# Products of an attention stage moved from 128 by 128 to 64 by 64 TensorE tiles, in a fused attention and feed-forward kernel

## The chip, the cores and the metric

The kernel runs on one core of one Trainium2 chip. A core has TensorE (PE; its weight loads are listed as PEld), VectorE (DVE), ScalarE (ACT), GpSimd (POOL) and SyncE (SP), which here only issues transfers. Each engine works through its own instructions in the order in which the program gives them. The metric is the device time of one execution in microseconds (us). A profiled execution leaves a trace; times of single instructions come from it.

## The reference

Eight batches of eight heads, 576 positions, 64 features each. q is normalised by a softmax over the features, k by one over the positions; kv = k^T v is a 64 by 64 matrix per head, and the attention's output is q kv. The heads' outputs side by side form x, 4608 rows by 512. Then comes a feed-forward part with a sine:

```python
k_s = np.exp(k - max_over_seq(k)); k_s = k_s / sum_over_seq(k_s)
q_s = np.exp(q - max_over_d(q));   q_s = q_s / sum_over_d(q_s)
kv = np.einsum('bhsd,bhse->bhde', k_s, v)
attn = np.einsum('bhsd,bhde->bhse', q_s, kv)
x = attn.transpose(0, 2, 1, 3).reshape(4608, 512)
h = x @ w_in                       # 512 by 2048
g = h + np.sin(alpha * h)**2 / (alpha + 1e-9)
out = g @ w_out                    # 2048 by 512
```

Inputs and output are float32 in HBM.

## The kernel before

**Feed-forward part.** The 4608 rows are worked through in nine tiles t of 512 rows. A tile has 16 slots (ni), one for each 128 columns of h. In a slot, `mm_h` makes four products of 128 by 512 (one for each 128-row chunk ki of w_in) into one PSUM bank, written hp; `sine` has ScalarE take the sine of it and the square; `combine` has VectorE form g from the square and from hp, which leaves the bank free. A later slot that is given the same bank waits for that combine. The order of the banks is written out: `BANKS` for tiles 0 to 2, and "aabb" repeated after that, where a and b are pools of two banks each. Each 512-row tile then needs 64 products with w_out (`mm_o`, four accumulations of 16), which `o_stream` hands out one by one: between two slots of tile t, `take(os, n)` puts n products of tile t-1 on TensorE's queue. After each 16 of them `evac_o` has VectorE copy the result out of PSUM and SP store it.

**Attention part.** While tile t = b-1 is worked through (for t from 3 to 6), batch b is prepared between its slots: exps of q and k on ScalarE before slot 0; normalising q on GpSimd; the transposed q (`qT`) by a transfer at slot 3; at slot 5 `kv_mm` with 72 small products on 64 by 64 tiles, then `kv_norm` on VectorE; and at slots 9, 11, 13 and 15 the products x = q kv (`attn_out`), each with a copy by VectorE into `xT`, the transposed x from which `mm_h` reads. xT is a ring of 2560 columns. Earlier batches are prepared in stretches of their own, with `attn_chunk`: batch 0 at the start, batch 1 after tile 0, batch 2 after tile 1; batch 3 is prepared in tile 2. A position s is j + 9p, with nine j of 64 positions.

**The x products before.** The 64 by 64 kv matrices of two heads stand on the diagonal of a 128 by 128 matrix (`kbd`), whose other blocks are set to zero once. One product of the full array then makes a chunk of x for two heads, of which half of the multiplications are by zeros. A batch has four chunks c = (ii, e) of 576 columns. `attn_out` makes the two chunks of one ii for four or five j: two products of 256 or 320 columns and one VectorE copy of 512 or 640 columns.

Of the kernel before, what the change touches and what calls it, by code (L numbers as in the profile page):

```python
# [15 lines left out]
F32 = mybir.dt.float32  # L16
BF16 = mybir.dt.bfloat16
AX = mybir.ActivationFunctionType
ALU = mybir.AluOpType
# [4 lines left out]
def kernel(  # L24
# [14 lines left out]
    nc = tc.nc  # L39
    ctx.enter_context(nc.allow_non_contiguous_dma(reason="layout"))  # L40
    B, H, S, D = q.shape
# [3 lines left out]
    J = 9  # L45
    P = S // J
    nN = d_ff // 128
    MF = 512
# [3 lines left out]
    NX = 5 * MF  # L52

    ctx.enter_context(tc.manual_schedule())
    singles = ctx.enter_context(tc.tile_pool(name="singles", bufs=1))
# [12 lines left out]
    xT = singles.tile([128, 4, NX], BF16, name="xT")  # L68
    q8 = singles.tile([128, 4, 2, D], F32, name="q8")
    win = singles.tile([128, 4, d_ff], BF16, name="win")  # L70
# [1 line left out]
    alpha_rows = singles.tile([nN, 128], F32, name="alpha_rows")  # L72
    alpha_sb = singles.tile([128, nN], F32, name="alpha_sb")
    inva_sb = singles.tile([128, nN], F32, name="inva_sb")
    kbd = [singles.tile([128, 2, 2, 128], BF16, name=f"kbd{n}") for n in range(2)]
    vb = [singles.tile([128, J, 4 * 65], BF16, name=f"vb{n}") for n in range(2)]

    def src_view(t, b):
        return t[b].rearrange("(i e) (p j) d -> (e p) i (j d)", e=2, j=J)

    win_v = moe_w_in.rearrange("(x c d) n -> x d c n", x=2, c=4)
    wout_v = moe_w_out.rearrange("(no ni) d -> ni no d", ni=128)
    out_v = out.rearrange("(b p j) d -> b j p d", b=B, j=J)

# [30 lines left out]
    A = {}  # L115
# [48 lines left out]
    def kv_mm(b, ii, pool, split=False):  # L164

        if ii == 0 or split:
            A["kvp", b] = pool.tile([128, 2, 512], F32, name="kvp", tag="a")
        kvp, ke, vt = A["kvp", b], A["ke", b], vb[b % 2]
        for j in range(J):
            for x in range(2):  # L170
                h = 2 * ii + x
                for e in range(2):
                    r = slice(64 * e, 64 * e + 64)
                    nc.tensor.matmul(kvp[64 * x:64 * x + 64, e, ii * 65:(ii + 1) * 65],  # L174
                                     ke[r, j, h * 64:(h + 1) * 64],
                                     vt[r, j, h * 65:(h + 1) * 65],
                                     start=(j == 0), stop=(j == J - 1))

    def kv_norm(b, i0=0, i1=2):

        kt, m = kbd[b % 2], i1 - i0
        kvr = small.tile([128, 2, 2], F32, name="kvr")[:, :, 0:m]
        src = A["kvp", b][:, :, i0 * 65:i1 * 65].rearrange("p e (ii c) -> p e ii c", ii=m)
        nc.vector.reciprocal(kvr, src[:, :, :, D])
        for x in range(2):
            r = slice(64 * x, 64 * x + 64)
            nc.vector.tensor_tensor(kt[r, :, i0:i1, r], src[r, :, :, 0:D],  # L187
                                    kvr[r].unsqueeze(3).to_broadcast([64, 2, m, D]), op=ALU.mult)

    def q_tile(b):  # L190
        if ("qT", b) not in A:
# [20 lines left out]
                in_ = in_.rearrange("p j c -> p (j c)")  # L212
            nc.sync.dma_start(out=out, in_=in_, transpose=True)

    XO = ((0, 4), (4, 9))

    def attn_out(b, ii, half, pool, eng):
        qT, kt = A["qT", b], kbd[b % 2]
        j0, j1 = XO[half]
        n = (j1 - j0) * P  # L220
        xp = pool.tile([128, 2, 512], F32, name="xp", tag="a")
        for e in range(2):
            nc.tensor.matmul(xp[:, e, 0:n], kt[:, e, ii], qT[:, ii, j0:j1, e * 64:(e + 1) * 64],  # L223
                             start=True, stop=True)
        c0 = (J * b + j0) * P % NX
        eng(xT[:, 2 * ii:2 * ii + 2, c0:c0 + n], xp[:, :, 0:n])  # L226

    def attn_chunk(b, c, j0, j1, xp):

        ii, e = divmod(c, 2)  # L230
        nc.tensor.matmul(xp, kbd[b % 2][:, e, ii], A["qT", b][:, ii, j0:j1, e * 64:(e + 1) * 64],
                         start=True, stop=True)


    G = {}

    HP = {}
    BANKS = {0: "aabbkllaabbkllaa", 1: "kbbllaakbbllaabb", 2: "aabbooaabbooaabb"}

    def bank(kind):  # L240

        if kind == "k":
            return ps_k.tile([128, 2, MF], F32, name="kvp", tag="a")[:, 0]
        pool = {"a": lambda: ps_h[0], "b": lambda: ps_h[1], "l": lambda: ps_l, "o": lambda: ps_o}[kind]()
        return pool.tile([128, MF], F32, name={"l": "lp", "o": "op"}.get(kind, "hp"), tag=kind)

    def mm_h(t, ni, k0=0, k1=4):

        if ni == 0 and k0 == 0:
            G[t] = gpool.tile([128, nN, MF], BF16, name="g")  # L250
        hp = HP[t, ni] if k0 else bank(BANKS.get(t, 4 * "aabb")[ni])
        HP[t, ni] = hp
        for ki in range(k0, k1):
            nc.tensor.matmul(hp, win[:, ki, ni * 128:(ni + 1) * 128],  # L254
                             xT[:, ki, t * MF % NX:t * MF % NX + MF], start=(ki == 0), stop=(ki == 3))
        return hp

    def sine(t, ni, hp, sq):
# [48 lines left out]
    zero = singles.tile([128, 1], F32, name="zero")  # L307
    nc.vector.memset(zero, 0.0)
    for n in range(2):
        nc.vector.memset(kbd[n], 0.0)  # L310
        nc.vector.memset(vb[n].rearrange("p j (i c) -> p j i c", i=4)[:, :, :, D:D + 1], 1.0)

    ps_h = [ctx.enter_context(tc.tile_pool(name=f"ps_{n}", bufs=2, space=PSUM, reuse_waits="tile")) for n in "ab"]
# [67 lines left out]
    cast_v0(1, 5, 9, DVE_CP)  # L381

    xp = [bank("b") for _ in range(2)]
    for c in range(2):
        attn_chunk(0, c, 0, 8, xp[c])
    DVE_CP(xT[:, 0, 0:MF], xp[0])
    ACT_CP(xT[:, 1, 0:MF], xp[1])
    ACT_CP(A["qT", 0][:, 1, 0:8], tp1)
    nc.scalar.activation(zero, zero, AX.Sin)
    kv_mm(0, 1, ps_k, split=True)  # L390
# [1 line left out]
    for ki in range(2):  # L392
        for ni in range(2):
            mm_h(0, ni, ki, ki + 1)
    for c in range(2, 4):
        xp = bank("l")
        attn_chunk(0, c, 0, 8, xp)
        DVE_CP(xT[:, c, 0:MF], xp)
    for ki in range(2):
        for ni in range(2, 4):  # L400
            mm_h(0, ni, ki, ki + 1)
# [21 lines left out]
    def take(it, n=1000):  # L423
        for _ in range(n):
            if next(it, 0) == 0:
                return
# [4 lines left out]
    with ES:  # L431
# [47 lines left out]

        def x_half(ii):  # L480
            xp = [bank("a") for _ in range(2)]
            for e in range(2):
                attn_chunk(1, 2 * ii + e, 0, 8, xp[e])
            for e in range(2):
                (ACT_CP, DVE_CP)[e](xT[:, 2 * ii + e, MF:2 * MF], xp[e])

        kv_mm(1, 0, ps_k, split=True)
        kv_norm(1, 0, 1)
# [23 lines left out]
        def late_q8(ni):  # L512
            if ni == 11:
                tp = ps_k.tile([128, 2, 2, 128], BF16, name="tp", tag="a")
                for b in range(2):
                    for ii in range(2):
                        nc.tensor.transpose(tp[:, ii, b], A["qe", 1][:, J - 2 + b, ii * 128:(ii + 1) * 128], identb)
                DVE_CP(A["qT", 1][:, :, J - 2:J], tp)
            elif ni == 15:
                xp = ps_k.tile([128, 4, 2, P], F32, name="xp", tag="a")  # L520
                for c in range(4):
                    ii, e = divmod(c, 2)
                    for b in range(2):
                        nc.tensor.matmul(xp[:, c, b], kbd[b][:, e, ii],
                                         A["qT", 1][:, ii, J - 2 + b, e * 64:(e + 1) * 64], start=True, stop=True)
                DVE_CP(xT[:, :, 16 * P:18 * P], xp.rearrange("p c b n -> p c (b n)"))

        for ni in range(nN):
            h_slot(1, ni, SQ[ni], lag)
# [33 lines left out]
    norm_q(3, [GP])  # L563
    take(os, 20)

    c0 = J * 2 * P
    for c in range(4):
        xp = bank("aabb"[c])[:, 0:6 * P]
        attn_chunk(2, c, 0, 6, xp)
        (ACT_CP, DVE_CP)[c % 2](xT[:, c, c0:c0 + 6 * P], xp)  # L570
        take(os, 3 if c == 1 else 1)
    xp = ps_a.tile([128, 2, 512], F32, name="xp", tag="a")[:, :, 0:6 * P]
    for c in range(4):
        attn_chunk(2, c, 6, 9, xp[:, c // 2, (c % 2) * 3 * P:(c % 2 + 1) * 3 * P])
    DVE_CP(xT[:, :, c0 + 6 * P:c0 + 9 * P].rearrange("p (h c) n -> p h c n", h=2),
           xp.rearrange("p h (c n) -> p h c n", c=2))
    take(os)
    q_transpose_dma(3)
    load_batch(4)

    def attn_back(b, n, engs=4 * (DVE_CP,), xs=(4, 6, 8, 10)):
        if n == 0:
            kv_mm(b, 0, ps_a)
            kv_mm(b, 1, ps_a)
            kv_norm(b)
        elif n in xs:
            m = xs.index(n)
            attn_out(b, m // 2, m % 2, ps_a, engs[m])

    SQ2 = "PAPPAPAPPAPAPPAP"  # L590
    for ni in range(nN):
        h_slot(2, ni, SQ2[ni], lag)
        flush(lag, 2)
        attn_back(3, ni - 5, (DVE_CP, ACT_CP, ACT_CP, DVE_CP), (4, 6, 8, 10))
    flush(lag, 0)

    for t in range(3, nT):
        b = t + 1 if t + 1 < B else None
        os = o_stream(t - 1)
        done = 0  # L600
        if b is not None:

            exp_q(b)
            exp_k(b)
            cast_v(b, [GP_CP, GP_CP])
            norm_q(b, [GP])
            take(os, 8)
            done = 8
        for ni in range(nN):
            hp = mm_h(t, ni)  # L610
            if b is not None:
                if ni == 3:
                    q_transpose_dma(b)
                    if b + 1 < B:
                        load_batch(b + 1)
                attn_back(b, ni - 5)
            s = sine(t, ni, hp, "A")
            combine(t, ni, hp, s)
            want = 23 + 2 * (t == 3) + 21 * ni // 8 if b is not None else 4 * (ni + 1)
            take(os, min(64, want) - done)  # L620
            done = min(64, want)
        take(os)
# [36 lines left out]
```

## Time and profile before

| | us |
|---|---|
| median of three runs | 284.75 |
| the three runs | 284.06, 284.75, 286.88 |
| the profiled execution | 283.85 |
| its span, first to last instruction | 282.1 |

| stretch of the span, us | length | TensorE busy | VectorE | ScalarE | GpSimd |
|---|---|---|---|---|---|
| start, 0 to 16 | 16.00 | 9.81 | 10.32 | 11.33 | 9.91 |
| batch 1 in preparation, 36 to 46 | 10.00 | 9.66 | 8.44 | 6.61 | 0.95 |
| batch 2 in preparation, 66 to 75.9 | 9.90 | 9.85 | 9.69 | 7.39 | 7.06 |
| tile 2, 75.9 to 93.3 | 17.40 | 17.24 | 13.14 | 15.29 | 12.28 |
| one loop of tiles 3 to 6, 178.93 to 208.35 | 29.42 | 29.16 | 20.51 | 27.30 | 4.21 |
| tile 7, 208.35 to 236 | 27.65 | 27.49 | 14.97 | 20.83 | 0.00 |

How to read it: busy times of engines overlap, so a row does not add up to its length. A line of a group or of a timeline names the engine, the source line, the operation, what it writes and reads, the shape and the count; an entry in brackets is the time for which the engine stood idle before it, and what ended that. Products on TensorE are pipelined: a record of a 512-column product lasts 0.379 us, while a new one starts every 0.217 us. The granted clock of TensorE is 1.00 in every stretch but the last. Some products have no record.

### The profile page before, as it was taken

Reading aid. Unit: us, or ns where it says so; the run is one execution under the profiler, and the core shown is the slowest. Engines: PE = TensorE matmul, PEld = TensorE weight load, DVE = VectorE, ACT = ScalarE, POOL = GpSimd, SP = SyncE. Lnnn points to the kernel's source line nnn. Section 1 sums busy time; section 2 is a strip of 40 time slices with the busy share of each in tenths; the row PEclk is TensorE's granted clock in tenths of the full one; section 3 lists DMA queues with packets and bytes.
Section 4 is the critical chain, followed back from the end, with each engine's and each line's share of the span. In section 5 each row is a group of like instructions: output and inputs, shape, how many; then the busy total and the mean of one; then the engine's idle time right before and its main releaser. Section 6 shows DMA issues by size and latency. Waiting matters only on the chain.

```text
span 282.1 us, 4812 instructions
## 1 busy us (share of the span) xinstructions
PE 270.1 (96%) x1826; PEld 128.0 (45%) x1855; DVE 188.7 (67%) x288; ACT 225.5 (80%) x322; POOL 83.8 (30%) x80
## 2 busy tenths in 40 slices
PE   1999999999999999999999999999999999999994
PEld 0444444444444444444444444444444444444443
DVE  3968768899967768766875677567775555555412
ACT  3989576999589999899989998999877777777400
POOL 1988421877676550115003500340000000000000
PEclk9999999999999999999999999999999999999998
DMA  7999999996599039811992099109011111111143
GB/s 252 310 173 221 280 332 322 358 345 243 124 224 393 10 68 329 305 37 38 266 386 50 22 283 388 27 18 160 6 34 37 37 40 37 37 38 43 42 104 74
DMA packets 39127, 45.80 MB, mean 162 GB/s; under 512 B 17072, under 2 KB 22464, under 8 KB 39104
## 3 DMA queue, kind: packets, MB, share of 16 engines
q1 hardware_dynamic: 33360, 40.57, 46.9%
q0 software_dynamic: 5552, 4.79, 10.4%
q8 instruction: 14, 0.23, 0.3%
q10 hardware_dynamic: 192, 0.14, 0.2%
q14 instruction: 9, 0.07, 0.1%
HBM read 36.71 MB, written 9.44 MB: 164 GB/s over the span
## 4 chain that ended last, share of the span: by engine, by line
PE 84%; DMA 6%; ACT 3%; DVE 2%; POOL 1%; issue 1%; SPq 1%; ACTq 0%
PE op L274 38%; PE hp L254 37%; DMA st_v<-in_v_dram 6%; PE xp L223 2%; PE kvp L174 2%; PE lp L254 2%; POOL s L264 1%; PE op L629 1%; PE op L254 1%; ACT s L260 1%; PE kvp L254 1%; ACT vb L329 1%; DVE g L270 1%; SPq L299 1%; SPq L445 0%
## 5 line engine op out<-in xcount | busy, mean ns | idle before, releaser
L270 DVE SCALAR_TENSOR_TENSOR g<-s,inva_sb,hp 128x512 bf16<-128x512 f32 x128 | 94.1, 745 | 58.1 <-ACT s L262 52.6
L254 PE MATMUL hp<-xT,win 128*128 128x512 bf16 x507 | 127.9, 379 | 0.4
L274 PE MATMUL op<-wout,g 128*128 128x512 bf16 x477 | 121.6, 379 | 1.4 <-issue 0.6
L260 ACT ACTIVATE s<-hp,alpha_sb 128x512 f32<-128x512 f32 x128 | 86.3, 682 | 22.9 <-PE hp L254 21.2
L254 PEld LDWEIGHTS <-win 128*128 128x128 bf16 x576 | 56.0, 98 | 67.5 <-issue 1.3
L274 PEld LDWEIGHTS <-g 128*128 128x128 bf16 x560 | 54.0, 98 | 61.0 <-DVE g L270 0.3
L262 ACT ACTIVATE s<-s 128x512 f32<-128x512 f32 x112 | 70.5, 630 | 3.5
L264 POOL TENSOR_TENSOR s<-s 128x512 f32<-128x512 f32 x29 | 30.4, 1063 | 20.0 <-ACT s L260 19.9
L153 POOL TENSOR_TENSOR qn<-qe,qs 128x1152 bf16<-128x1152 bf16 (+1 forms) x12 | 25.1, 2109 | 34.1 <-DVE qs L147 22.7
L286 DVE COPY o<-op 128x512 f32<-128x512 f32 (+2 forms) x33 | 22.1, 668 | 9.9 <-PE op L274 5.5
L138 POOL CAST vb<-st_v 128x1152 bf16<-128x1152 f32 x12 | 14.7, 1257 | 45.3 <-DMA st_v<-in_v_dram 45.3
L119 ACT ACTIVATE qe<-st_q 128x1152 bf16<-128x1152 f32 (+2 forms) x18 | 17.7, 1025 | 6.7 <-DMA st_q<-in_q_dram 6.6
L119 ACT ACTIVATE ke<-st_k 128x1152 bf16<-128x1152 f32 x16 | 17.9, 1151 | 1.2 <-DMA st_k<-in_k_dram 1.2
L146 DVE TENSOR_REDUCE qs<-qe 128x36 f32<-128x2304 bf16 x5 | 12.8, 2553 | 7.9 <-ACT qe L119 7.9
L226 DVE CAST xT<-xp 128x512 bf16<-128x512 f32 (+1 forms) x18 | 13.5, 749 | 0.0
L119 ACT ACT_TABLE_LOAD x7 | 9.0, 1283 | 1.3 <-PEq L643 1.2
L274 PE MATMUL lp<-wout,g 128*128 128x512 bf16 x31 | 8.8, 379 | 0.2 <-issue 0.2
L274 PE MATMUL hp<-wout,g 128*128 128x512 bf16 x30 | 8.6, 379 | 0.1
L223 PE MATMUL xp<-qT,kbd 128*128 128x256 bf16 (+1 forms) x40 | 8.2, 286 | 0.0
L174 PEld LDWEIGHTS <-ke 64*64 64x64 bf16 x576 | 5.8, 108 | 4.6 <-ACT ke L119 0.8
L187 DVE TENSOR_TENSOR kbd<-kvp,kvr 64x256 bf16<-64x256 f32 (+1 forms) x20 | 7.4, 369 | 0.5
L254 PE MATMUL lp<-xT,win 128*128 128x512 bf16 x30 | 7.5, 379 | 0.1
(86 smaller groups left out, 135.0 us busy)
## 6 DMA issues: line engine op xcount, KB each, us to landing
out_dram<-o SPq DMA_DIRECT2D x70, 128.0 KB, 2.4
st_q<-in_q_dram SPq DMA_DIRECT2D x6, 1152.0 KB, 6.7
st_k<-in_k_dram SPq DMA_DIRECT2D x6, 1152.0 KB, 8.8
st_v<-in_v_dram SPq DMA_DIRECT2D x6, 1152.0 KB, 11.4
st_k<-in_k_dram SPq DMA_DIRECT2D x4, 576.0 KB, 7.5
st_q<-in_q_dram SPq DMA_DIRECT2D x4, 512.0 KB, 6.1
st_v<-in_v_dram SPq DMA_DIRECT2D x3, 576.0 KB, 8.0
wout<-in_moe_w_out_dram POOLq DMA_DIRECT2D x3, 512.0 KB, 10.3
```

The source lines that it names most:

```text
L119: nc.scalar.activation(dst[:, :, ii * 128:(ii + 1) * 128].rearrange("p j (x d) -> p x j d", x=2), src[:, ii::2], AX.Exp)
L138: engs[ii](vv[:, 2 * ii:2 * ii + 2, :, 0:D], staged["v", b][:, ii::2])
L153: engs[ii % len(engs)].tensor_tensor(qn[:, ii, 0:j1].rearrange("p j (x d) -> p j x d", x=2), qe[:, ii], part.unsqueeze(3).to_broadcast([12 ...
L223: nc.tensor.matmul(xp[:, e, 0:n], kt[:, e, ii], qT[:, ii, j0:j1, e * 64:(e + 1) * 64], start=True, stop=True)
L226: eng(xT[:, 2 * ii:2 * ii + 2, c0:c0 + n], xp[:, :, 0:n])
L254: nc.tensor.matmul(hp, win[:, ki, ni * 128:(ni + 1) * 128], xT[:, ki, t * MF % NX:t * MF % NX + MF], start=(ki == 0), stop=(ki == 3))
L260: nc.scalar.activation(s, hp, AX.Sin, scale=alpha_sb[:, ni:ni + 1])
L262: nc.scalar.activation(s, s, AX.Square)
L264: nc.gpsimd.tensor_tensor(s, s, s, op=ALU.mult)
L270: nc.vector.scalar_tensor_tensor(G[t][:, ni], in0=s, scalar=inva_sb[:, ni:ni + 1], in1=hp, op0=ALU.mult, op1=ALU.add)
L274: nc.tensor.matmul(acc, G[t][:, ni, j * 128:(j + 1) * 128], wout[:, ni, :], start=(ni == 0), stop=(ni == nN - 1))
L286: eng(o[:, cols], acc)
```

## The change

- `kbd` holds the two kv matrices above each other, 128 by 64 for each (e, ii), without zeros; `kv_norm` is one VectorE instruction on 128 partitions in place of two on 64, and the memsets of kbd go.
- `attn_x` makes x with four products on 64 by 64 tiles, one for each half x of the rows and each e of the columns. The two row halves write into two banks. The chunks of x are thereby other pairs of heads: chunk 2x+ii holds e = 0 and 1. The rows of w_in are loaded in the order that goes with it, and `KO` has `mm_h` take the chunks in the order in which they are made.
- Eight of the nine j make 512 columns, one bank. The ninth is made by `last_j` apart: eight products of 64 columns and one VectorE copy.
- Batches 4 to 7: the x products of slots 9, 11, 13 and 15 become one group of eight at slot 11. Its four banks are the two of pool a, lent, and the two of the pool that kv and x have used. Slots 12 and 13 use pool b in place of a, so the order of banks from slot 8 on is a a b b b b a a, for all tiles from 3 on. The copies are four VectorE instructions of 512 columns, two at slot 11, one each at slots 12 and 13; where the ring ends inside a batch (batch 4), each is split into two. The ninth group of batches 3 to 6 is made at slot 5 of the next loop, directly behind kv, in a part of kv's bank; that of batch 7 at slot 14.
- Batch 3 has a group of four at slots 9 and 13, batch 2 two groups of four (the second with the ninth group), batch 1 two and batch 0 two; the first of batch 0 stands directly ahead of a kv.

In the built program, VectorE's order in tiles 4 to 6 is: combine of slot 10, an output copy, two x copies, combine of slot 11, an x copy, combine of slot 12, an x copy, combine of slot 13. In tile 3 the output copy stands ahead of the combine of slot 10, and the x copies are twice as many. The first product of slot 12 waits for the combine of slot 10, that of slot 13 for the combine of slot 11. The orders of GpSimd and of SP are as before.

```diff
-    kbd = [singles.tile([128, 2, 2, 128], BF16, name=f"kbd{n}") for n in range(2)]
+    kbd = [singles.tile([128, 2, 2, D], BF16, name=f"kbd{n}") for n in range(2)]
-    win_v = moe_w_in.rearrange("(x c d) n -> x d c n", x=2, c=4)
+    win_v = moe_w_in.rearrange("(c x d) n -> x d c n", x=2, c=4)
...
-        for x in range(2):
-            r = slice(64 * x, 64 * x + 64)
-            nc.vector.tensor_tensor(kt[r, :, i0:i1, r], src[r, :, :, 0:D],
-                                    kvr[r].unsqueeze(3).to_broadcast([64, 2, m, D]), op=ALU.mult)
+        nc.vector.tensor_tensor(kt[:, :, i0:i1], src[:, :, :, 0:D],
+                                kvr.unsqueeze(3).to_broadcast([128, 2, m, D]), op=ALU.mult)
...
+    def attn_x(b, ii, j0, j1, outs):
+
         for e in range(2):
-            nc.tensor.matmul(xp[:, e, 0:n], kt[:, e, ii], qT[:, ii, j0:j1, e * 64:(e + 1) * 64],
-                             start=True, stop=True)
+            for x in range(2):
+                r = slice(64 * x, 64 * x + 64)
+                nc.tensor.matmul(outs[x][64 * e:64 * e + 64], kbd[b % 2][r, e, ii],
+                                 A["qT", b][r, ii, j0:j1, e * 64:(e + 1) * 64], start=True, stop=True)
...
+    def x_copy(eng, c, b, xp):
+
+        n0 = min(8 * P, NX - J * b * P % NX)
+        for n, m in ((0, n0), (n0, 8 * P)):
+            if n < m:
+                d0 = (J * b * P + n) % NX
+                eng(xT[:, c, d0:d0 + m - n], xp[:, n:m])
+
+    def last_j(b, xn):
+
+        for ii in range(2):
+            attn_x(b, ii, J - 1, J, [xn[:, x, ii * P:(ii + 1) * P] for x in range(2)])
...
+    KO = (0, 2, 1, 3)
...
-        hp = HP[t, ni] if k0 else bank(BANKS.get(t, 4 * "aabb")[ni])
+        hp = HP[t, ni] if k0 else bank(BANKS.get(t, 3 * "aabb" + "bbaa")[ni])
...
-        nc.vector.memset(kbd[n], 0.0)
...
+    def attn_kv(b):
+
+        kv_mm(b, 0, ps_a)
+        kv_mm(b, 1, ps_a)
+        if b > 3:
+            xn = A["kvp", b][:, :, 256:512]
+            last_j(b - 1, xn)
+        kv_norm(b)
+        if b > 3:
+            last_j_copy(b - 1, xn)
...
-        attn_back(3, ni - 5, (DVE_CP, ACT_CP, ACT_CP, DVE_CP), (4, 6, 8, 10))
+        if ni == 5:
+            attn_kv(3)
+        elif ni in (9, 13):
+            x_pair(3, ni // 12, pair(), (DVE_CP, ACT_CP))
...
-                attn_back(b, ni - 5)
+                if ni == 5:
+                    attn_kv(b)
+                elif ni == 11:
+                    xh, xa = [bank("a") for _ in range(2)], pair()
+                    attn_x(b, 0, 0, 8, xh)
+                    attn_x(b, 1, 0, 8, xa)
+                    for x in range(2):
+                        x_copy(DVE_CP, 2 * x, b, xh[x])
+                elif ni in (12, 13):
+                    x_copy(DVE_CP, 2 * (ni - 12) + 1, b, xa[ni - 12])
+                if b == B - 1 and ni == 14:
+                    xn = ps_a.tile([128, 2, 512], F32, name="xp", tag="a")
+                    last_j(b, xn)
+                    last_j_copy(b, xn)
```

More of the change, by code (lines that the diff above doesn't have):

```diff
@@ L213, in q_transpose_dma, with x_cols, last_j_copy @@
             nc.sync.dma_start(out=out, in_=in_, transpose=True)
[L215 to L221, printed above, removed]
-        for e in range(2):
-            nc.tensor.matmul(xp[:, e, 0:n], kt[:, e, ii], qT[:, ii, j0:j1, e * 64:(e + 1) * 64],
-                             start=True, stop=True)
-        c0 = (J * b + j0) * P % NX
[L226 to L232, printed above, removed]
+    def attn_x(b, ii, j0, j1, outs):
+        for e in range(2):
+            for x in range(2):
+                r = slice(64 * x, 64 * x + 64)
+                nc.tensor.matmul(outs[x][64 * e:64 * e + 64], kbd[b % 2][r, e, ii],
+                                 A["qT", b][r, ii, j0:j1, e * 64:(e + 1) * 64], start=True, stop=True)
+    def x_cols(b, j0, j1):
+        c0 = (J * b + j0) * P % NX
+        return slice(c0, c0 + (j1 - j0) * P)
+    def x_copy(eng, c, b, xp):
[7 more added lines that the diff above has]
+            attn_x(b, ii, J - 1, J, [xn[:, x, ii * P:(ii + 1) * P] for x in range(2)])
+    def last_j_copy(b, xn):
+        DVE_CP(xT[:, :, x_cols(b, J - 1, J)].rearrange("p (x i) n -> p x i n", x=2),
+               xn[:, :, 0:2 * P].rearrange("p x (i n) -> p x i n", i=2))
+    KO = (0, 2, 1, 3)
     G = {}
@@ L250, in mm_h @@
             G[t] = gpool.tile([128, nN, MF], BF16, name="g")
-        hp = HP[t, ni] if k0 else bank(BANKS.get(t, 4 * "aabb")[ni])
+        hp = HP[t, ni] if k0 else bank(BANKS.get(t, 3 * "aabb" + "bbaa")[ni])
         HP[t, ni] = hp
-        for ki in range(k0, k1):
-            nc.tensor.matmul(hp, win[:, ki, ni * 128:(ni + 1) * 128],
-                             xT[:, ki, t * MF % NX:t * MF % NX + MF], start=(ki == 0), stop=(ki == 3))
+        for k in range(k0, k1):
+            nc.tensor.matmul(hp, win[:, KO[k], ni * 128:(ni + 1) * 128],
+                             xT[:, KO[k], t * MF % NX:t * MF % NX + MF], start=(k == 0), stop=(k == 3))
         return hp
@@ L383 @@
     xp = [bank("b") for _ in range(2)]
-    for c in range(2):
-        attn_chunk(0, c, 0, 8, xp[c])
+    attn_x(0, 0, 0, 8, xp)
     DVE_CP(xT[:, 0, 0:MF], xp[0])
-    ACT_CP(xT[:, 1, 0:MF], xp[1])
+    ACT_CP(xT[:, 2, 0:MF], xp[1])
     ACT_CP(A["qT", 0][:, 1, 0:8], tp1)
@@ L394 @@
             mm_h(0, ni, ki, ki + 1)
[L395 to L398, printed above, removed]
+    xp = [bank("l") for _ in range(2)]
+    attn_x(0, 1, 0, 8, xp)
+    for x in range(2):
+        DVE_CP(xT[:, 2 * x + 1, 0:MF], xp[x])
     for ki in range(2):
@@ L481, in x_half @@
             xp = [bank("a") for _ in range(2)]
[L482 to L485, printed above, removed]
+            attn_x(1, ii, 0, 8, xp)
+            for x in range(2):
+                (ACT_CP, DVE_CP)[x](xT[:, 2 * x + ii, MF:2 * MF], xp[x])
         kv_mm(1, 0, ps_k, split=True)
@@ L519, in late_q8 @@
             elif ni == 15:
-                xp = ps_k.tile([128, 4, 2, P], F32, name="xp", tag="a")
-                for c in range(4):
-                    ii, e = divmod(c, 2)
+                xp = ps_k.tile([128, 2, 512], F32, name="xp", tag="a")
+                for ii in range(2):
                     for b in range(2):
-                        nc.tensor.matmul(xp[:, c, b], kbd[b][:, e, ii],
-                                         A["qT", 1][:, ii, J - 2 + b, e * 64:(e + 1) * 64], start=True, stop=True)
-                DVE_CP(xT[:, :, 16 * P:18 * P], xp.rearrange("p c b n -> p c (b n)"))
+                        for e in range(2):
+                            for x in range(2):
+                                r, c = slice(64 * x, 64 * x + 64), (2 * ii + b) * P
+                                nc.tensor.matmul(xp[64 * e:64 * e + 64, x, c:c + P], kbd[b][r, e, ii],
+                                                 A["qT", 1][r, ii, J - 2 + b, e * 64:(e + 1) * 64],
+                                                 start=True, stop=True)
+                DVE_CP(xT[:, :, 16 * P:18 * P].rearrange("p (x i) n -> p x i n", x=2),
+                       xp[:, :, 0:4 * P].rearrange("p x (i n) -> p x i n", i=2))
         for ni in range(nN):
@@ L564 @@
     take(os, 20)
[L566 to L576, printed above, removed]
+    for ii in range(2):
+        xp = [bank("ab"[ii]) for _ in range(2)]
+        attn_x(2, ii, 0, 8, xp)
+        if ii == 1:
+            xn = ps_a.tile([128, 2, 512], F32, name="xp", tag="a")
+            last_j(2, xn)
+        for x in range(2):
+            x_copy((ACT_CP, DVE_CP)[x], 2 * x + ii, 2, xp[x])
+        take(os, 4)
+    last_j_copy(2, xn)
     take(os)
@@ L579, with x_pair, pair @@
     load_batch(4)
[L581 to L588, printed above, removed]
+    def x_pair(b, ii, xp, engs):
+        attn_x(b, ii, 0, 8, xp)
+        for x in range(2):
+            x_copy(engs[x], 2 * x + ii, b, xp[x])
+    def pair():
+        t = ps_a.tile([128, 2, 512], F32, name="xp", tag="a")
+        return [t[:, x] for x in range(2)]
+    def attn_kv(b):
[7 more added lines that the diff above has]
+            last_j_copy(b - 1, xn)
     SQ2 = "PAPPAPAPPAPAPPAP"
@@ L615 @@
                         load_batch(b + 1)
-                attn_back(b, ni - 5)
+                if ni == 5:
[4 more added lines that the diff above has]
+                    attn_x(b, 1, 0, 8, xa)
+                    for x in range(2):
+                        x_copy(DVE_CP, 2 * x, b, xh[x])
+                elif ni in (12, 13):
+                    x_copy(DVE_CP, 2 * (ni - 12) + 1, b, xa[ni - 12])
+                if b == B - 1 and ni == 14:
+                    xn = ps_a.tile([128, 2, 512], F32, name="xp", tag="a")
+                    last_j(b, xn)
+                    last_j_copy(b, xn)
             s = sine(t, ni, hp, "A")
```

## The prediction

> **What bounds the kernel now.** I read the page from the top: busy shares, then the chain of waits, then timelines of single stretches. Two lines of the page settle who sets the time.
>
> ```profile
> PE 270.1 (96%) x1826; PEld 128.0 (45%) x1855; DVE 188.7 (67%) x288; ACT 225.5 (80%) x322; POOL 83.8 (30%) x80
> ...
> PE 84%; DMA 6%; ACT 3%; DVE 2%; POOL 1%; issue 1%; SPq 1%; ACTq 0%
> ```
>
> TensorE is busy for 96% of the span and is 84% of the chain, so a product saved on TensorE is time saved, and a wait added there is time lost, unless another wait swallows it. The other shares are averages; what matters is how far VectorE and ScalarE lie behind TensorE in each stage, which only a timeline tells.
>
> The first stretch is the kv stage of batch 3, TensorE alone (columns: start us, us, engine, line, operation). It prices 64 by 64 tiles, for kv already runs on them.
>
> ```profile
> 79.17 1.89 PE L254 MATMUL op<-xT,win 128*128 128x512 bf16 x8
> 80.99 0.81 PE L174 MATMUL kvp<-vb,ke 64*64 64x65 bf16 x72
> 81.73 3.63 PE L254 MATMUL hp<-xT,win 128*128 128x512 bf16 x15
> 85.20 0.38 PE L223 MATMUL xp<-qT,kbd 128*128 128x256 bf16 x2
> 85.41 1.89 PE L254 MATMUL op<-xT,win 128*128 128x512 bf16 x8
> ```
>
> From 81.73 to 85.20 lie sixteen products (one record is missing): 0.217 us per 512 columns. Eight from 79.17 end at 80.90, and kv starts at 80.99: 0.09 to go into the small tiles. One kv record lasts 0.193, so the last of 72 starts at 81.61: 0.62 for 71 steps, 8.7 ns each. The next big product starts 0.12 later, of which 0.03 is the streaming of 65 columns: 0.09 to come out. A visit to the small tiles thus costs 0.18.
>
> The second stretch is the sixth tile loop (t=6, batch 7 in preparation), around slot 11 of 16.
>
> ```profile
> 199.44 1.03 PE L254 MATMUL hp<-xT,win 128*128 128x512 bf16 x4
> ...
> 200.51 0.69 ACT L260 ACTIVATE s<-hp,alpha_sb 128x512 f32<-128x512 f32 x1 [0.17 <-PE hp L254]
> ...
> 200.96 1.03 PE L254 MATMUL hp<-xT,win 128*128 128x512 bf16 x4
> 201.23 0.63 ACT L262 ACTIVATE s<-s 128x512 f32<-128x512 f32 x1
> ...
> 201.82 0.43 PE L223 MATMUL xp<-qT,kbd 128*128 128x320 bf16 x2
> 201.89 0.75 DVE L270 SCALAR_TENSOR_TENSOR g<-s,inva_sb,hp 128x512 bf16<-128x512 f32 x1 [0.77 <-ACT s L262]
> ...
> 202.55 0.68 DVE L286 COPY o<-op 128x512 f32<-128x512 f32 x1
> ...
> 203.16 0.81 DVE L226 CAST xT<-xp 128x640 bf16<-128x640 f32 x1
> ...
> 203.89 0.74 DVE L270 SCALAR_TENSOR_TENSOR g<-s,inva_sb,hp 128x512 bf16<-128x512 f32 x1
> 204.03 1.03 PE L254 MATMUL hp<-xT,win 128*128 128x512 bf16 x4
> ```
>
> The four lines of hp are slots 10, 11 and (last) 13. Slot 10's product has streamed at 200.31 (start plus four times 0.217), its sine starts 0.20 later, its combine (L270) at 201.89. Slot 11's combine starts only at 203.89, behind an output copy and an x copy. Slot 13 starts at 204.03, before that combine is over (204.63): it may, since it uses a bank that slot 9 left long ago. VectorE starts back-to-back work before the record of the last is over: 0.66 after a combine, 0.61 after a 0.68 copy.
>
> **The change, part by part.** I call T the moment at which slot 11's product has streamed (201.82 above).
>
> Small tiles, price of a group. Four products of 512 columns on four tiles at once: 0.217 plus three steps of 8.7 ns is 0.24, with the visit 0.42. Two full-size products cost 0.43. So a group of four alone gains nothing. Eight at once: 0.46 and 0.18 is 0.64, against 0.87. The ninth group beside kv needs no visit: eight products at 8.7 ns are 0.07. No row shows 512 columns on small tiles. Bounds: 0.24 for four if all stream together, 0.87 if they take turns. I take 0.24, for kv puts 4680 columns through in 0.62 us, 7.5 per ns, where one stream does 2.36.
>
> The Trainium skill (TensorEngine Tiling (Array Packing), Key Properties) says that changing the tiling mode drains TensorE; the 0.09 on either side of kv is what this trace shows of it. Without the drain, batch 3's two groups and batch 7's last one would be 0.54 us cheaper together, and the sum 0.8 in place of 1.3; the visits at slot 11 hide in the wait worked out below.
>
> Batches 4 to 7, TensorE's own work. Before, x takes 0.22 at slots 9 and 13 (204.90 to 205.12 in the same answer) and 0.27 at slots 11 and 15 (201.82 to 202.09, 207.92 to 208.19): 0.98. After: 0.64 at slot 11 and 0.07 with kv at slot 5. That is 0.27 less in each loop; in t=6 the ninth group of batch 7 has a visit of its own, 0.25 more.
>
> Batches 4 to 7, the lent banks. Slots 12 and 13 now use the two banks of slots 10 and 11, so slot 13 must wait for slot 11's combine. VectorE takes in order: combine 10, output copy, two x copies, combine 11. For t=4 to 6: combine 10 starts at T+0.07; then 0.66, 0.61, 0.61, 0.61 and combine 11's own 0.745 end at T+3.31. A signal from VectorE reaches TensorE in 0.06 (kbd ends 44.49, L231 starts 44.55): T+3.37. TensorE itself would be there at T plus 0.64 (x), 0.43 (two output products), 0.87 (slot 12), 0.65 (three) = T+2.59. A new wait of 0.78; in line behind it stand the output products and slots 14 and 15. Slot 12 needs combine 10 (T+0.82) and comes at T+1.07: no wait. Before, slot 13 came at T+2.21. So each loop gains 3.37 - 2.21 = 1.16, loses 0.71 (x at 9, 13, 15), gains 0.07: +0.52, and t=6 +0.77. Whatever x costs up to 1.42 is hidden in that wait.
>
> In t=3 the output copy falls one slot earlier, but the ring ends inside batch 4 and each x copy is split: four of 256 columns stand between the combines. The trace has 512 columns at 0.683 and 640 at 0.816, so I extrapolate 0.42, starts 0.35 apart (bounds 0.30 and 0.61). Combine 11 ends at T + 0.07 + 0.66 + 1.40 + 0.745 = 2.88, slot 13 at 2.94: a wait of 0.35 and +0.09 (up to +1.13).
>
> These four loops: 0.09 + 0.52 + 0.52 + 0.77 = +1.90. ScalarE ends each 0.27 later relative to TensorE, as x at slot 15 no longer covers it; in the next loop slot 4 starts at 160.36 where its combine ended at 159.71, 0.65 of cover, so that costs nothing. Tiles 7 and 8 have the same bank order: there a combine ends 2.33 after its product (222.22 to 224.55) and the second slot after it comes after three stretches of 0.87, 2.60: no wait, with 0.2 to spare.
>
> The Trainium skill (the same page, PSUM Bottleneck) warns that after a TensorE speedup the copies out of PSUM may become the limit, and advises ScalarE and VectorE together. The change puts all four copies on VectorE; by the rule, one of the two between the combines would go to ScalarE and the wait of 0.78 would be 0.17.
>
> Batches 0 to 3. kv_norm is one step in place of two of 0.29. In batch 1 TensorE waits for it twice: 41.12 to 41.23, and 44.32 (five products from 43.24) to 44.55, where kbd ended at 44.49: -0.33. In batch 0 ScalarE's copy of qT (ends 14.53) holds the second x pair anyway: 0. The memsets of kbd lie at 1.6 to 2.3 us, before the first input: 0. Batch 2: 0.98 before (four of 0.16, then 0.33), 0.42 + 0.49 after: -0.07. Batch 3: two groups of 0.42 for 0.98: -0.14. The late columns of batches 0 and 1: 0.34 before, sixteen steps and a visit, 0.32, after. w_in comes in the same pieces, and queues, orders of SP and POOL stay as they are: 0.
>
> **Sum.** +1.90 - 0.33 - 0.07 - 0.14 - 0.02 = +1.3. The profiled execution took 283.85 us (span 282.1), so 285.2; the median of the runs is 0.9 above it: 286.1.
>
> **Rivals.** (1) No wait: VectorE has combine 11 ready in time. Then the four loops are worth 4 x -0.27 + 0.25 = -0.83, the sum is -1.4: 283.4. It needs 0.78 off a queue of five steps; two x copies in half their time would nearly do it. Nothing in the rows shows that.
> (2) Clearly slower: ScalarE is not level with TensorE at slot 10. In the loop before (t=5) it first waits for TensorE at slot 8, by 0.16; its two steps take 1.25 and slot 10 now follows slot 9 by 1.30, as x at slot 9 is gone. Every delay of sine 10 passes through combines 10 and 11 into slot 13, four times. From 0.4 us on, the sum is above +2.9; at 0.5 it is +3.3: 288.1. The same comes from VectorE if it doesn't overlap its starts: record laid to record, combine 11 ends 0.30 later in three loops and 0.35 in t=3.
> (3) The tiles take turns: groups of four cost 0.87 + 0.18. Slot 13 then comes at T+3.86, 0.49 to 0.92 more in four loops, and some 0.6 for each of six earlier groups: about +7, 292. The kv rate speaks against it.
>
> **How the numbers follow.** The forecast, a wait near 0.8 in three loops, has 0.55; (1) 0.19; (2) 0.20; (3) 0.04; the rest 0.02. Likeliest time 286.1, by itself 285.2 to 287.3. The range for 8 in 10 reaches into (1) and (2): 283.0 to 289.0. One per cent, 2.85 us, is about what a measurement here can tell from no change. Slower by more holds most of (2), (3) and 0.06 of the forecast: 0.29. Faster by more would need twice what (1) gives: 0.05. Within: 0.66.
>
> **What would show it.** In the profile after: hp of slot 13 idle before it, released by VectorE's combine, about 0.8 long in three loops, 0.35 in t=3, and the two x copies directly ahead of that combine; the eight x products from first to last start 0.25 to 0.3 us apart; hp to x and back 0.09 each; loops t=4 and 5 0.5 longer. No such idle time means (1); sine 10 without idle time before it means (2); x products 0.2 apart mean (3). I would be wrong outright if batch 1 or the start moved by more than half a microsecond.

## The result and the profile after

The changed kernel takes 287.46 us in the median of eight runs (286.84 to 288.35), the kernel before, run beside it, 284.56: a ratio of 1.0105, 95% interval 1.0083 to 1.0127. It is slower by some 3 us, where 1.3 was forecast. The median lies inside the stated range of 283.0 to 289.0, and a little above the 285.2 to 287.3 that the forecast gave for its own mechanism. The profiled execution took 288.35 us, the slowest of the eight.

The page after, the two lines that answer to those of before:

```profile
PE 269.4 (94%) x1890; PEld 123.8 (43%) x1919; DVE 184.3 (64%) x285; ACT 225.4 (79%) x322; POOL 83.4 (29%) x80
...
PE 78%; DMA 7%; DVE 5%; ACT 5%; issue 2%; POOL 2%; SPq 0%; ACTq 0%
```

TensorE's share of the chain fell from 84% to 78%, and VectorE, ScalarE and transfers rose: TensorE now waits. (The 79% of ScalarE is 225.4 us as before.) To see where, I read from the timelines when certain work starts, and took differences. All times are us; kv(b) is the start of batch b's 72 small products. The last five columns belong to the experiments below.

| from | to | before | after | e1 | e2 | e3 | e4 | e5 |
|---|---|---|---|---|---|---|---|---|
| 0 | first w_out product | 28.50 | 29.79 | 28.93 | 28.18 | 28.70 | 28.51 | 29.34 |
| there | kv(3) | 52.49 | 52.46 | 52.63 | 52.40 | 52.40 | 52.40 | 52.62 |
| kv(3) | kv(4) | 23.37 | 24.79 | 23.13 | 24.65 | 24.65 | 23.13 | 23.13 |
| kv(4) | kv(5) | 29.02 | 29.11 | 29.11 | 28.86 | 29.11 | 28.87 | 28.87 |
| kv(5) | kv(6) | 29.44 | 29.91 | 29.91 | 29.20 | 29.91 | 29.19 | 29.19 |
| kv(6) | kv(7) | 29.43 | 29.89 | 29.88 | 29.17 | 29.88 | 29.17 | 29.17 |
| kv(7) | last 32 products | 82.63 | 83.40 | 83.39 | 84.06 | 83.39 | 84.06 | 82.76 |

After and e3 run the same instructions (e3 only loads w_in's rows in another order): from kv(4) on they agree to 0.01, so small differences there mean something; between the first w_out product and kv(4) they agree to 0.14. The first row scatters, by 1.09 between these two. Without it, after is 3.18 above before: 1.42 between kv(3) and kv(4), 1.02 in the next three rows, 0.77 in the last, -0.03 ahead of kv(3). That is the measured difference; the 1.29 of the first row belongs to this one execution.

**Slot 13, as forecast.** The timeline of the changed kernel, tile 4, slots 10 to 13 (start us, us, engine, line, operation; in brackets the idle time before):

```profile
144.74 1.03 PE L263 MATMUL hp<-xT,win 128*128 128x512 bf16 x4
...
145.67 0.75 DVE L279 SCALAR_TENSOR_TENSOR g<-s,inva_sb,hp 128x512 bf16<-128x512 f32 x1 [0.54 <-ACT s L271]
...
145.69 0.41 PE L218 MATMUL hp<-qT,kbd 64*64 64x512 bf16 x4
...
145.93 0.39 PE L218 MATMUL xp<-qT,kbd 64*64 64x512 bf16 x4
...
146.25 0.61 PE L283 MATMUL op<-wout,g 128*128 128x512 bf16 x2
146.34 0.68 DVE L295 COPY o<-op 128x512 f32<-128x512 f32 x1
...
146.94 1.28 DVE L231 CAST xT<-hp 128x512 bf16<-128x512 f32 x2
...
148.13 0.74 DVE L279 SCALAR_TENSOR_TENSOR g<-s,inva_sb,hp 128x512 bf16<-128x512 f32 x1
...
148.92 1.02 PE L263 MATMUL hp<-xT,win 128*128 128x512 bf16 x4 [0.56 <-DVE g L279]
```

T is 144.74 + 0.866 (four products) = 145.60. The group of eight starts at 145.69, its second half 0.24 after the first, and output products follow at 146.25: 0.65 from T, where 0.64 was worked out. The first four records span 0.41 together and last 0.400 each, so within a set of four the products start some 3 ns apart, and not the 8.7 ns of the prediction. Combine 11 (148.13) stands behind an output copy and two x copies; slot 13 starts at T+3.32, where 3.37 was worked out and TensorE's own queue would have been ready at T+2.61. The wait is 0.71 for the 0.78 worked out. (The 0.56 in brackets counts from the end of a record, which lasts longer than its product streams.)

**The start of tile 3, not forecast.** In the kernel before, ScalarE copied batch 3's x in tile 2 without idle time, and its table load came ahead of tile 3's first product:

```profile
88.60 0.67 ACT L226 CAST xT<-xp 128x640 bf16<-128x640 f32 x1
...
90.32 0.59 ACT L226 CAST xT<-xp 128x512 bf16<-128x512 f32 x1
...
92.76 1.28 ACT L119 ACT_TABLE_LOAD   x1
```

```profile
93.26 1.03 PE L254 MATMUL hp<-xT,win 128*128 128x512 bf16 x4
```

After, VectorE's copies of batch 3's x, then ScalarE's:

```profile
87.94 0.68 DVE L231 CAST xT<-xp 128x512 bf16<-128x512 f32 x1
...
92.31 0.68 DVE L231 CAST xT<-xp 128x512 bf16<-128x512 f32 x1
```

```profile
88.66 0.59 ACT L231 CAST xT<-xp 128x512 bf16<-128x512 f32 x1 [0.52 <-DVE xT L231]
...
93.03 0.59 ACT L231 CAST xT<-xp 128x512 bf16<-128x512 f32 x1 [0.79 <-DVE xT L231]
...
95.46 1.28 ACT L119 ACT_TABLE_LOAD   x1
```

and TensorE a little later, in tile 3:

```profile
94.39 1.03 PE L263 MATMUL hp<-xT,win 128*128 128x512 bf16 x4
...
97.39 2.33 PE L283 MATMUL op<-wout,g 128*128 128x512 bf16 x10 [0.47 <-DVE g L279]
...
104.57 1.02 PE L263 MATMUL hp<-xT,win 128*128 128x512 bf16 x4 [0.74 <-DVE g L279]
```

ScalarE stands still for 1.31 us although its half of x is ready: it waits for VectorE's copy of the other half, and starts 0.04 after that copy's end at 88.62 and at 92.99. Both copies read halves of one PSUM tile (`pair()` makes it, two banks wide), and the program has the second reader wait for the first; e1 below turns that wait round. Batch 1's copies go into xT as well but read two separate tiles, and those of its second group start together: ScalarE's at 46.24, VectorE's at 46.27. The table load that opens the exps then comes 1.07 after tile 3's first product (94.39); before it came 0.50 ahead of it (92.76 and 93.26). So sines and combines of the last slots of tile 2 and of slot 0 of tile 3 are late, and TensorE waits for both: slot 4 (104.57) has the bank of slot 0.

### The profile page after: what moved, and what is told of

The parts are those of the page before. It is cut to its first block, busy times and chain, and to the rows that moved or that the text cites. A ratio compares the mean times of both kernels' runs of the same rounds, so it can differ in the third digit from the quotient of the medians.

```text
span 286.6 us, 4937 instructions
## 1 busy us (share of the span) xinstructions
PE 269.4 (94%) x1890; PEld 123.8 (43%) x1919; DVE 184.3 (64%) x285; ACT 225.4 (79%) x322; POOL 83.4 (29%) x80
## 4 chain that ended last, share of the span: by engine, by line
PE 78%; DMA 7%; DVE 5%; ACT 5%; issue 2%; POOL 2%; SPq 0%; ACTq 0%
PE op L283 33%; PE hp L263 32%; DMA win<-in_moe_w_in_dram 3%; PE hp L283 2%; DVE g L279 2%; PE lp L283 2%; DVE xT L231 2%; PE kvp L174 2%; PE lp L263 2%; DMA st_v<-in_v_dram 2%; DMA st_k<-in_k_dram 2%; ACT s L269 2%; PE op L665 1%; DVE o L295 1%; PE kvp L263 1%
## 5 line engine op out<-in xcount | busy, mean ns | idle before, releaser
L283 PEld LDWEIGHTS <-g 128*128 128x128 bf16 x560 | 53.2, 98 | 65.4 <-issue 2.3
L174 PE MATMUL kvp<-vb,ke 64*64 64x65 bf16 x576 | 7.0, 194 | 1.2 <-ACT vb L337 1.2
L109 POOL DMA_DIRECT2D win<-in_moe_w_in_dram x12 | 7.4, 654 | 1.0 <-DMA win<-in_moe_w_in_dram 0.6
L151 DVE TENSOR_REDUCE qs<-qe 128x16 f32<-128x1024 bf16 (+1 forms) x4 | 5.1, 1266 | 3.4 <-ACT qe L119 3.4
```

Source lines behind the costliest of these rows:

```text
L283: nc.tensor.matmul(acc, G[t][:, ni, j * 128:(j + 1) * 128], wout[:, ni, :], start=(ni == 0), stop=(ni == nN - 1))
```

## The experiments

Theory: the loss is two separate waits, ScalarE's for VectorE's copy in tile 2 and slot 13's for combine 11. Rivals: ScalarE simply has more to do; the lent banks cost it whatever the order of the copies; the new row order of w_in slows the start; the small tiles are dearer than the records show.

**e1: batch 3's copies in the other order.**

```diff
-        for x in range(2):
+        for x in (1, 0):
             x_copy(engs[x], 2 * x + ii, b, xp[x])
```

> Batch 3's pairs in tile 2: ScalarE's x copy is issued ahead of VectorE's, nothing else. In the changed kernel ScalarE's copy waits for VectorE's copy of the same PSUM tile, 0.52 and 0.79 us, and TensorE then waits 0.47 and 0.74 us in tile 3 for combines that come from late sines. Theory (ScalarE late by that wait): both TensorE waits go, tile 3 is 1.2 to 1.5 us shorter, ratio to before about 1.005. Rival (ScalarE is late through the amount of its work): the TensorE waits stay, ratio stays near 1.0105. Rival (VectorE, which now waits for ScalarE's copy, takes the loss over): waits of TensorE for combines appear inside tile 2.

Measured: 285.78 against 284.35, ratio 1.0071 (1.0043 to 1.0099). The table shows 23.13 between kv(3) and kv(4) in place of 24.79 (24.65 in e3), and from there on the same as after. ScalarE, VectorE and TensorE of e1:

```profile
87.21 0.57 ACT L231 CAST xT<-xp 128x512 bf16<-128x512 f32 x1
...
90.66 0.58 ACT L231 CAST xT<-xp 128x512 bf16<-128x512 f32 x1
```

```profile
87.81 0.69 DVE L231 CAST xT<-xp 128x512 bf16<-128x512 f32 x1 [0.62 <-ACT xT L231]
```

```profile
94.42 3.83 PE L283 MATMUL op<-wout,g 128*128 128x512 bf16 x17
98.09 1.03 PE L263 MATMUL hp<-xT,win 128*128 128x512 bf16 x4
...
102.22 1.02 PE L263 MATMUL hp<-xT,win 128*128 128x512 bf16 x4
```

ScalarE does the same copies without idle time, and the entries behind TensorE's lines are gone. The amount of work is the same, only the wait moved to VectorE (0.62 at the first pair), which has time in tile 2: TensorE has no idle entry there. The ratio alone would not decide, for its interval overlaps that of the changed kernel; the rows do. The first theory stands, against both rivals to it.

**e2: the x copies of slots 11 to 13 behind the combine of their slot.**

```diff
                     attn_x(b, 1, 0, 8, xa)
-                    for x in range(2):
-                        x_copy(DVE_CP, 2 * x, b, xh[x])
-                elif ni in (12, 13):
-                    x_copy(DVE_CP, 2 * (ni - 12) + 1, b, xa[ni - 12])
...
             combine(t, ni, hp, s)
+            if b is not None and ni == 11:
+                for x in range(2):
+                    x_copy(DVE_CP, 2 * x, b, xh[x])
+            elif b is not None and ni in (12, 13):
+                x_copy(DVE_CP, 2 * (ni - 12) + 1, b, xa[ni - 12])
```

> Tiles 3 to 6: the x copies of slots 11 to 13 are issued behind the combine of their slot, nothing else. Theory (slot 13 waits for combine 11 behind two x copies): combine 11 ends 1.2 us earlier, slot 13 no longer waits (0.56 us idle in each of three loops, 0.71 late by its own queue), each of these loops is 0.7 shorter, in all about 2.1 us, ratio about 1.003. Rival (the lent banks themselves are the limit): the wait moves to slot 14 or 15, which now wait for the x copies, and the ratio stays above 1.008.

Measured: 285.59 against 284.35, ratio 1.0062 (1.0039 to 1.0084): less of a gain than the 1.003 expected, and an interval that reaches the rival's 1.008. The first three loops did what the theory says: 0.25, 0.71 and 0.72 less than after. Tile 4 of e2:

```profile
145.12 0.75 DVE L279 SCALAR_TENSOR_TENSOR g<-s,inva_sb,hp 128x512 bf16<-128x512 f32 x1 [0.16 <-ACT s L271]
...
145.79 1.28 DVE L231 CAST xT<-hp 128x512 bf16<-128x512 f32 x2
...
146.15 1.03 PE L263 MATMUL hp<-xT,win 128*128 128x512 bf16 x4
```

Combine 11 now starts right behind its square, and slot 13 (146.15) without idle time. But in tile 6, where batch 7's ninth group follows at slot 14 into the bank pair that holds the last x half, the edit made a new wait, at the slot that the rival names:

```profile
207.59 0.68 DVE L231 CAST xT<-xp 128x512 bf16<-128x512 f32 x1
...
208.33 0.26 PE L218 MATMUL xp<-qT,kbd 64*64 64x64 bf16 x8 [1.31 <-DVE xT L231]
```

That copy stands behind combine 13 now. The last row of the table has it: 84.06 in place of 83.40.

**e3: w_in's rows in the old order.** The edit is the one line of `win_v`, set back.

> w_in is loaded in the row order of the kernel before, so that h is made with w_in's rows in the wrong places; all else as in the changed kernel. In the changed kernel's trace the first pieces of w_in land in 6.0 us (median) in place of 4.8 and TensorE waits for them 0.69, 0.22 and 0.39 us, 1.3 us in all. Theory A (the new row order makes these transfers slower): the waits go and the time falls by about 1.3 us, ratio 1.006. Theory B (the landing times vary from execution to execution): landing times in the trace scatter with no tie to the order, the ratio stays within 0.002 of 1.0105.

Measured: 287.45 against 284.35, ratio 1.0120 (1.0096 to 1.0143), within the bound of theory B; the interval leaves out theory A's 1.006. In this profile TensorE waits for w_in nowhere, but neither does it in those of e2, e4, e5, e6 and e8, which have the new order; in those of e1 and e7 it does, for 0.7 and 0.5. The first w_out product comes between 28.18 and 29.34 in the eight profiles of experiments, at 28.50 in that of before. The 29.79 of after is the late end of a scatter in which four profiles with the new order, e2, e4, e6 and e8, come as early as before or nearly so (28.18 to 28.51).

**e4: e1 and e2 together.**

> The edits of e1 and e2 together. If both are separate losses they add: 3.0 - 1.4 - 2.1 us is 0.5 us below the kernel before, ratio 0.998. If they share a loss (a ScalarE that is less late, but TensorE waits at the same place), the sum is less than the parts and the ratio stays above 1.001.

Measured: 284.87 against 284.35, ratio 1.0023 (1.0007 to 1.0040), by the ratio what a shared loss would give. But row by row, e4 has e1's gain and e2's gains and e2's new wait: the losses are separate. What keeps it from 0.998 should then be the 1.31 at slot 14, which e5 takes up.

**e5: e4, and batch 7's ninth group one slot later.** It is emitted at slot 15, its copy behind combine 15.

> As e4_both, and the ninth group of batch 7 moves from slot 14 to slot 15, its copy behind the last combine. In e4_both the ninth group waited 1.3 us at slot 14 for an x copy that e2's edit had moved behind combine 13 (the same bank pair). Theory: that wait is the whole of what e4 still lost, from the kv of batch 7 to the end takes 82.7 us as before the change (84.06 in e4), ratio 0.998. Rival: the wait follows the group to slot 15, or the next tile's first product waits for the copy, and the ratio stays at 1.002.

Measured: 283.45 against 284.19, ratio 0.9967 (0.9952 to 0.9982). From kv(7) to the end it takes 82.76. This version beats the changed kernel and, by 0.3 per cent, the one before, and its chain shows TensorE again:

```profile
PE 86%; DMA 5%; ACT 3%; POOL 1%; SPq 1%; DVE 1%; issue 1%; ACTq 0%
```

**e6: small tiles without lent banks.** Two groups of four at slots 9 and 13 in all loops, the old order of banks, e1's order in batch 3.

```diff
-                elif ni == 11:
...
+                elif ni in (9, 13):
+                    x_pair(b, ni // 12, pair(), (DVE_CP, DVE_CP))
```

> Small tiles without lent banks: batches 4 to 7 take two groups of four at slots 9 and 13 in the two banks that kv uses, copies by VectorE, the old order of banks; the ninth group stays with kv, that of batch 7 at slot 15; batch 3 with ScalarE's copy first. Theory (a group of four on small tiles costs 0.44, two full products 0.43 to 0.49): each loop is worth 0.44 + 0.44 + 0.07 for 0.98, about 0, no new wait; with batch 3's 0.2 the ratio is 0.999 to 1.001. Rival (small tiles cost more than the groups show, through later weight loads or waits): loops 0.3 or more longer than before, ratio above 1.004.

Measured: 284.17 against 284.19, ratio 1.0007 (0.9984 to 1.0031). The three loops from kv(4) to kv(7) take 29.10, 29.43 and 29.39, before 29.02, 29.44 and 29.43. Small tiles by themselves are worth nothing here in groups of four; the group of eight pays for its visit (28.87, 29.19 and 29.17 in e5).

**e7: sixteen more groups of four.**

```diff
+            if t == 7:
+                if ni == 0:
+                    xv = pair()
+                attn_x(7, ni % 2, 0, 8, xv)
             s = sine(t, ni, hp, "A")
```

> The changed kernel with sixteen more groups of four products of 512 columns on small tiles in tile 7, one in each slot behind the h product, whose results nobody reads. Theory (four stream together, a visit costs 0.18 on top): 0.42 to 0.44 a group, 6.7 to 7.0 us in all. If they took turns it would be 1.05 a group, 16.8 us; without the cost of a visit 0.24, 3.8 us. The products themselves start 8 to 9 ns apart.

Measured: 294.61 against 284.19, ratio 1.0364 (1.0334 to 1.0393): 7.15 above the changed kernel's median, 0.45 a group. The traces agree: from kv(7) to the last 32 products e7 takes 90.54, after 83.40, 7.14 more. TensorE of e7:

```profile
214.50 1.03 PE L263 MATMUL hp<-xT,win 128*128 128x512 bf16 x4
215.45 0.41 PE L218 MATMUL xp<-qT,kbd 64*64 64x512 bf16 x4
215.79 1.04 PE L283 MATMUL op<-wout,g 128*128 128x512 bf16 x4
```

The h products end at 214.50 + 0.866 = 215.37; 0.08 later the group starts, and 0.34 after that the next full-size product. Four streams of 512 columns run at once (in turn they would take 0.87), with 0.2 around them. The four products start within 0.01, some 3 ns apart, and not 8 to 9.

**e8: one of slot 11's copies given to ScalarE, on top of e1.**

> As e1_act_first, and at slot 11 of tiles 3 to 6 ScalarE makes the second of the two x copies in place of VectorE, ahead of the sine of slot 11 in its own order. By the prediction's sentence on the rule to use both engines, the wait of slot 13 falls by one copy, 0.6 us in each of three loops, ratio 1.001. Against it: ScalarE is in order too; its copy starts about 0.56 after T and lasts 0.59, so sine and square of slot 11 end at T+2.5 in place of T+1.55, combine 11 starts at T+2.53, as late as before, and the ratio stays at e1's 1.007.

Measured: 285.73 against 284.25, ratio 1.0050 (1.0030 to 1.0070); the interval leaves out the first forecast, 1.001, and ends at the second, 1.007. The trace is plainer. Tile 4:

```profile
143.51 0.59 ACT L231 CAST xT<-hp 128x512 bf16<-128x512 f32 x1 [0.54 <-PE hp L218]
...
145.38 0.75 DVE L279 SCALAR_TENSOR_TENSOR g<-s,inva_sb,hp 128x512 bf16<-128x512 f32 x1 [0.43 <-ACT s L271]
...
146.18 1.02 PE L263 MATMUL hp<-xT,win 128*128 128x512 bf16 x4 [0.48 <-DVE g L279]
```

With T at 142.94, combine 11 starts at T+2.44 (after: T+2.53), and its idle entry now names ScalarE. Two loops are 0.08 and 0.07 shorter than e1's 29.91 and 29.88, and the one of tile 3 is 0.46 longer (29.57 for 29.11), as ScalarE gets two copies there too. The wait of slot 13 stays: taking a copy off VectorE's queue was of no use here, since ScalarE's copy held up its own sine.

## Why the prediction was right, and where it was not

- *Price of a group, right in size.* Worked out 0.42 for four and 0.64 for eight; measured 0.42 to 0.45 (tile 2 and e7) and 0.65. The streams run together; the rival of taking turns is out. The step of 8.7 ns was misread: it is the mean over kv's 72 products, and in the trace these come in sets of four that start within 0.01, the first at 80.99, the next at 81.05. The step hardly weighs in the sum.
- *Batches 4 to 7 and the lent banks, right in mechanism and size.* Forecast +0.09, +0.52, +0.52 and +0.77; measured +0.09, +0.47, +0.46 and +0.77. e2 takes the cause away, and the first three loops drop to 0.16, 0.24 and 0.26 below before, where the rival without a wait had 0.27 for each.
- *Split copies of tile 3, right.* Extrapolated 0.42 for 256 columns; the records show 0.414.
- *"Batch 3: two groups of 0.42 for 0.98: -0.14": this is the step that failed.* It priced TensorE alone. Between kv(3) and kv(4) +1.42 was measured. The change gave the two halves of one PSUM tile to two engines, and I did not ask whether the second copy waits for the first. e1 brings that stretch to -0.24 with no other edit. The prediction's second rival had ScalarE's lateness as a loss, but at slot 10 of the loops. There it is level: in tile 4 sine 10 starts at 144.29, 0.20 after its product has streamed (143.22 + 0.866), the same 0.20 as in the kernel before. The sign named for that rival, no idle time before sine 10, does appear there, so it was no sign of lateness. The lateness came from a wait in tile 2 and was paid in tile 3.
- *Batch 1, the same fault in small.* Forecast -0.33, again for TensorE alone; from the first w_out product to tile 1's first product it gained 0.15 (17.14 to 16.99), and tile 1 gave back 0.14. The traces suggest where it went, though no run tests it. Of the two waits for kbd that were to go, the second did; in place of the first, 0.11, stands the way into the small tiles, 0.10 (42.46 to 42.56), and the transposes behind it start 0.05 after ScalarE's copy of x ends, before as after (42.24 and 42.29; 43.60 and 43.65). Tile 1 follows ScalarE: its first sine starts 19.10 and 19.07 after the first w_out product, so what TensorE gains ahead of it would turn into waiting.
- *Batch 2 and the late columns, as forecast:* -0.02 for -0.07 from tile 1's output products to kv(3), and 0.34 before against 0.34 after, the way in included.
- *The start.* By its own last sign the prediction would be wrong outright if the start moved by more than half a microsecond. In the profile of after it moved by 1.29, but the first row of the table scatters by as much between runs that differ in nothing there, so that sign can't be read from one profile.
- *The rule to use both engines.* The prediction worked out 0.17 for slot 13's wait by the Trainium skill's advice (TensorEngine Tiling (Array Packing), PSUM Bottleneck). In e8 slot 13 is still 0.64 late by TensorE's own queue (0.71 in after), since the sine that combine 11 needs queues behind ScalarE's copy. Here the order of the copies decided, not their number per engine.
- *The drain between tilings.* The same page's statement (Key Properties) fits the 0.08 to 0.10 on the way in and a similar time on the way out; in e6 these visits eat the whole gain of streaming four at once. No run tells a drain from another cost of the switch.

The sum, 1.3 forecast, 3.0 measured. By the rows of the table the forecast is -0.42 ahead of kv(3), -0.14 for batch 3 and +1.90 behind it; measured are -0.03, +1.42 and +1.79. So 1.56 of what is missing is batch 3's copy, 0.39 the stretch ahead of it (mostly batch 1), and the loops give back 0.11. That the median still lies inside the range is luck in part: the range reached up for a late sine 10 or a VectorE that does not overlap its starts, neither of which came, and the loss that filled the room was not among the rivals. At 1.05 per cent, interval 0.83 to 1.27, the result lies on the one per cent at which the prediction divided its chances, and does not settle the side.

## What to carry to other kernels

Products on small tiles share one change of tiling, so group them until their saving exceeds it (here 0.45 for 0.43 with four, 0.65 for 0.87 with eight), and price the visit from a place where the kernel already makes one. When banks are lent, follow the next owner's wait back through the releasing engine's queue in order: here the same copies, issued behind a combine in place of ahead of it, made three loops 0.16 to 0.26 shorter than before the change in place of 0.09 to 0.47 longer. And when one PSUM tile is read by two engines, look in the built program whether the second reader waits for the first, and let the engine with no time to spare go first.

## What the runs showed of the hardware that I had not expected

A product of 512 columns on a small tile has a record of 0.400 us where one on the full array has 0.379, though four of them pass in 0.24 and start some 3 ns apart. The landing of w_in at the start varies from profile to profile: from 4.8 to 6.6 us from issue in the median of its twelve transfers, with the first w_out product at 28.19 for 4.8 and at 29.79 for 6.6. A difference of 1 us in the first 30 us of a single profile of this kernel can't be put down to a change.
